# Attention products two groups at a time, an ordered exponential and two store queues in a two-layer transformer kernel

## The chip, the cores and the metric

The kernel runs on one core of a Trainium2 chip. The time is device time in microseconds (us) from the first to the last instruction of the slowest core, as reported for each run; the profile's own span is about 1.7 us shorter. Engine names are those of the profile: PE is TensorE, PEld its weight loads, DVE is VectorE, ACT is ScalarE, POOL is GpSimd, SP is SyncE. A "q" behind a name means the engine's sequencer, for example one that issues a DMA.

## The reference, cut to what matters

```python
def _A_ref(x, wqkv, wo):                  # S=2048, D=1024, H=32 heads of Dh=32
    W, dil = 8, 2                         # each position sees itself and 7 earlier ones, 2 apart
    q, k, v = ...                         # from x @ wqkv
    logits = einsum("bhsd,bhswd->bhsw", q, k at idx) * scale
    attn = _softmax(where(mask, logits, -1e9), axis=-1)
    o = einsum("bhsw,bhswd->bhsd", attn, v at idx)
    return o @ wo

def _B_ref(x, W_gate, W_up, W_down):      # F=3584
    gate = relu(x @ W_gate); up = x @ W_up
    return (gate * up) @ W_down

for _ in range(2):
    x = x + _A_ref(_layernorm(x), ...)
    x = x + _B_ref(_layernorm(x), ...)
```

The products of the sliding-window attention run on VectorE, the large matrix products on TensorE. The kernel cuts the 2048 positions into four blocks of 512 and treats two layer pairs times four blocks as eight "blocks", n = 0 to 7. While TensorE does the gate/up and down products of block n, VectorE does the attention of block n+1.

## The kernel before

Four things matter. First, the gate/up steps. In step j (28 of them per block) TensorE fills one accumulator for the gate and one for the up product. Accumulators lie in PSUM, the memory that TensorE writes its sums to; it is divided into banks. ScalarE turns the gate accumulator into `r`. VectorE multiplies it with the up accumulator into `hT`. An accumulator is free for TensorE again only when its reader is done. There are six of them (`tag="acc"`), and each is one PSUM bank in the compiled program.

```python
psum = ctx.enter_context(tc.tile_pool(name="psum", bufs=6, space=bass.MemoryType.PSUM))
# ... cut
for nm in ("g", "u"):
    acc = psum.tile([P, BLK], F32, tag="acc", name=f"acc_{nm}")
    with pe_group():
        for kc in range(KC):
            mm(acc[:], ...)
    accs[nm] = acc
    if nm == "g":
        r = pool["hid"].tile([P, BLK], BF16, tag="r", name="r", bufs=3)
        tail_act[0] = nc.scalar.activation(r[:], acc[:], ACT.Relu).ins
dv(nc.vector.tensor_tensor, hold["hT"][:, j, :], accs["u"][:], r[:], op=ALU.mult)
```

Second, the attention products. Eight groups per block, four VectorE instructions each, and each instruction needs the one before it:

```python
tt = work.tile([P, W, DG, P], BF16, tag="t", name=f"pv_{n}_{g}")
# ... cut: a_bc and v_sh are views of the softmax and of v
dv(nc.vector.tensor_tensor, tt[:], a_bc, v_sh, op=ALU.mult)
dv(nc.vector.tensor_tensor, tt[:, 0:4], tt[:, 0:4], tt[:, 4:8], op=ALU.add)
dv(nc.vector.tensor_tensor, tt[:, 0:2], tt[:, 0:2], tt[:, 2:4], op=ALU.add)
dv(nc.vector.tensor_tensor, ohm[:, g * DG:(g + 1) * DG, :], tt[:, 0], tt[:, 1], op=ALU.add)
gate[0] = tail_dve[0]
```

Third, the helper `dv`: every VectorE instruction given through it is issued after the one given before (`issue_after` fixes the order; it is not a wait). So the hT products and the attention groups stand in one fixed order, that of the planned times at which the Python code emits them. Instructions that do not go through such a helper are placed by the scheduler of the framework. In the kernel before, the exponential of the softmax was one of these:

```python
nc.scalar.activation(d[:], d[:], ACT.Exp, scale=scale)
```

Fourth, DMAs given through `sp_dma` stand in one order on SyncE's queue. `o_d` is the attention result as it is stored, `oT` the same loaded back in the shape that the output projection needs, `w_o` the weights of that projection, `xnT_b` the transposed input of the gate/up products.

## Time and profile before

| | before |
|---|---|
| time, median of the first 3 runs | 1626.2 us (1625.94 to 1627.49) |
| span of the profiled run | 1624.3 us |
| TensorE, VectorE, ScalarE busy | 99%, 68%, 31% |
| end of the last matmul to the end of the span | 3.3 us |

This is the line of the page for the kernel before with the busy time of each engine, its share of the span and the number of instructions:

```profile
PE 1615.9 (99%) x7618; PEld 785.2 (48%) x7618; DVE 1100.5 (68%) x939; ACT 502.2 (31%) x1051; POOL 250.2 (15%) x220
```

TensorE is the limit, but 99% says little about what is left to gain: the Trainium skill ("Perfetto Trace Analysis", Identifying the Most-Contended Engine) warns that the busy share of pipelined matmuls is a poor measure. A sharper reading takes the start times of all 7618 matmuls, in order, and adds up whatever exceeds the steady pace. For 512 columns this pace is 0.216 us. Beyond the start-up, very little exceeds it. The waits view of the kernel before, for PE alone, has the same events with smaller numbers (each line: who waited, for whom, us in total, times, longest):

```profile
PE acc_g L129 <- DVE hT L103: 1.2, 4, 0.3
PE acc_wo L129 <- DMA oT<-o_d: 0.3, 1, 0.3
PE acc_u L129 <- DVE hT L103: 0.2, 1, 0.2
```

Measured from start to start, each of these six waits costs 0.41 to 0.48 us rather than 0.2 to 0.3. In the profile a matmul of 512 columns lasts 0.379 us, while the next one normally starts 0.216 us after it; the difference, 0.16 us of every loss, lies under the record of the matmul before and does not count as idle there.

The chain of waits (followed back from the last instruction, shares of the span by engine) puts much more on VectorE:

```profile
PE 88%; DVE 10%; issue 1%; DMA 1%; ACT 0%; POOL 0%; DVEq 0%; SPq 0%
```

This must not be read as 10% to be won. The chain passes through VectorE wherever TensorE waited for it, even for 0.3 us, and then follows VectorE's own past for 20 us and more, while TensorE was at work all that time.

Why is hT late? These are lines of VectorE's timeline in the gate/up stage of block 1, others left out (start in us, duration, engine, instruction; in square brackets the idle time before it and what ended it):

```profile
352.13 0.68 DVE L103 TENSOR_TENSOR hT<-acc_u,r 128x512 bf16<-128x512 f32 x1
357.96 1.91 DVE L103 TENSOR_REDUCE ssum<-d 128x128 f32<-128x1024 f32 x1 [5.15 <-ACT d L600]
362.64 2.28 DVE L103 TENSOR_TENSOR pv<-a,vhm 128x4096 bf16<-128x4096 bf16 x1
364.96 1.95 DVE L103 TENSOR_TENSOR pv<-pv 128x2048 bf16<-128x2048 bf16 x2
366.95 0.42 DVE L103 TENSOR_TENSOR ohm<-pv 128x512 bf16<-128x512 bf16 x1
378.37 1.28 DVE L103 TENSOR_TENSOR hT<-acc_u,r 128x512 bf16<-128x512 f32 x2
```

VectorE stands idle for 5.15 us until the exponential (written to `d`) is done. Then it works through groups of 4.65 us with hT products in between. The hT product that starts at 378.37 ends at 379.06, too late for TensorE, which stops until 379.11:

```profile
379.11 1.89 PE L129 MATMUL acc_g<-xnT_b,w_g 128*128 128x512 bf16 x8 [0.31 <-DVE hT L103]
```

### The profile page before, as it was taken

The page shows a single profiled execution, that of the slowest core. Times are in us where ns is not written, and L with a number is a line of the kernel's source. Part 1 is how long each engine was busy: PE and PEld are TensorE (multiplying, and loading weights), DVE is VectorE, ACT ScalarE, POOL GpSimd, SP SyncE. Part 2 cuts the span into 40 slices and gives each one's busy share as a digit, 9 for nine tenths or more (in the row PEclk, how much of TensorE's full clock was granted, in tenths as well). Part 3 has the DMA queues.
Part 4 walks back from the last instruction along what each step waited for, and adds up shares of the span by engine and source line. Part 5 has one row for each costly group of instructions (what it writes and reads, how often), then busy time and mean ns, then how long its engine had stood idle before and what let it go on. Part 6 is the DMA issues. An engine that isn't in the chain of part 4 may idle for free.

```text
span 1624.3 us, 18771 instructions
## 1 busy us (share of the span) xinstructions
PE 1615.9 (99%) x7618; PEld 785.2 (48%) x7618; DVE 1100.5 (68%) x939; ACT 502.2 (31%) x1051; POOL 250.2 (15%) x220
## 2 busy tenths in 40 slices
PE   9999999999999999999999999999999999999999
PEld 6644445444544445444454444544445444444444
DVE  5799899959496777928679286892858928511211
ACT  5754322325240513405134051330513311131110
POOL 2411003201350102201052010520105100000000
PEclk9999999999999999999999999999999999999999
DMA  9579556776579485694757948579574894655451
GB/s 303 105 192 260 167 171 198 194 207 181 156 216 228 155 228 185 182 229 149 226 179 188 241 148 227 160 204 250 164 230 154 200 251 158 207 164 174 156 168 66
DMA packets 398006, 309.39 MB, mean 190 GB/s; under 512 B 167648, under 2 KB 377952, under 8 KB 396256
## 3 DMA queue, kind: packets, MB, share of 16 engines
q1 hardware_dynamic: 397632, 307.81, 67.1%
q8 instruction: 59, 0.97, 0.2%
q10 hardware_dynamic: 288, 0.39, 0.1%
q14 instruction: 27, 0.22, 0.0%
HBM read 263.06 MB, written 27.29 MB: 179 GB/s over the span
## 4 chain that ended last, share of the span: by engine, by line
PE 88%; DVE 10%; issue 1%; DMA 1%; ACT 0%; POOL 0%; DVEq 0%; SPq 0%
PE acc_g L129 21%; PE acc_u L129 20%; PE dacc L129 18%; PE acc_wo L129 7%; PE acc_q L129 6%; DVE pv L103 6%; PE dacc_pair L129 6%; PE acc_k L129 5%; PE acc_v L129 5%; DVE hT L103 1%; DVE ssum L103 1%; DMA x<-in_A_x_dram 1%; DVE prod L103 1%; DVE bst L103 0%; ACT d L600 0%
## 5 line engine op out<-in xcount | busy, mean ns | idle before, releaser
L129 PE MATMUL acc_g<-xnT_b,w_g 128*128 128x512 bf16 x1792 | 423.3, 379 | 1.2 <-DVE hT L103 1.2
L129 PE MATMUL acc_u<-xnT_b,w_u 128*128 128x512 bf16 x1792 | 423.3, 379 | 0.2 <-DVE hT L103 0.2
L711 ACT ACTIVATE r<-acc_g 128x512 bf16<-128x512 f32 x224 | 133.4, 595 | 751.8 <-PE acc_g L129 722.3
L103 DVE TENSOR_TENSOR hT<-acc_u,r 128x512 bf16<-128x512 f32 x224 | 150.0, 687 | 237.7 <-PE acc_u L129 235.5
L129 PE MATMUL dacc<-w_d,hT 128*128 128x512 bf16 (+1 forms) x1400 | 301.6, 375 | 0.0
L129 PEld LDWEIGHTS <-hT 128*128 128x128 bf16 x1820 | 178.2, 98 | 208.9
L129 PEld LDWEIGHTS <-w_g 128*128 128x128 bf16 x1792 | 175.2, 98 | 213.6 <-issue 3.0
L129 PEld LDWEIGHTS <-w_u 128*128 128x128 bf16 x1792 | 175.4, 98 | 211.8 <-issue 0.5
L547 DVE TENSOR_TENSOR t<-q,k 128x2048 f32<-128x2048 bf16 x84 | 191.8, 2292 | 8.7 <-ACT k L482 5.8
L557 DVE TENSOR_TENSOR ac<-ac,t 128x2048 f32<-128x2048 f32 x84 | 191.9, 2285 | 0.3
L103 DVE TENSOR_TENSOR pv<-a,vhm 128x4096 bf16<-128x4096 bf16 x64 | 146.1, 2283 | 0.0
L487 POOL COPY kh<-k 128x14 bf16<-128x14 bf16 x64 | 80.0, 1254 | 398.7 <-ACT k L482 398.7
L748 DVE TENSOR_TENSOR x<-dacc,x 128x512 bf16<-128x512 f32 (+1 forms) x50 | 32.1, 676 | 158.1 <-PE dacc L129 158.1
L103 DVE TENSOR_TENSOR pv<-pv 128x2048 bf16<-128x2048 bf16 (+1 forms) x128 | 122.7, 959 | 4.4
L129 PE MATMUL acc_wo<-w_o,oT 128*128 128x512 bf16 x512 | 111.9, 379 | 0.3 <-DMA oT<-o_d 0.3
L246 POOL TENSOR_TENSOR st_a<-st_a,neg_half 128x1 f32<-128x1 f32 x32 | 49.4, 1551 | 390.7 <-ACT st_a L245 390.7
L129 PE MATMUL dacc_pair<-w_d,hT 128*128 128x512 bf16 x420 | 95.9, 379 | 0.0
L246 POOL TENSOR_TENSOR st_b<-st_b,neg_half 128x1 f32<-128x1 f32 x29 | 47.6, 1650 | 289.9 <-ACT st_b L245 289.9
L129 PEld LDWEIGHTS <-oT 128*128 128x128 bf16 x512 | 49.7, 97 | 61.2 <-DMA oT<-o_d 0.8
L486 POOL COPY k<-kh 128x14 bf16<-128x14 bf16 x48 | 67.5, 1406 | 68.4 <-DVE t L547 43.8
L478 ACT CAST q<-acc_q 128x512 bf16<-128x512 f32 x64 | 37.3, 583 | 75.3 <-PE acc_q L129 75.3
L241 ACT ACTIVATE xn_b<-x 128x1024 bf16<-128x1024 bf16 x29 | 30.3, 1046 | 93.0 <-DVE x L687 78.0
(137 smaller groups left out, 1232.2 us busy)
## 6 DMA issues: line engine op xcount, KB each, us to landing
w_g<-in_B_W_gate_dram SPq DMA_DIRECT2D x56, 1024.0 KB, 6.7
w_u<-in_B_W_up_dram SPq DMA_DIRECT2D x56, 1024.0 KB, 5.5
w_d<-in_B_W_down_dram SPq DMA_DIRECT2D x48, 1024.0 KB, 5.8
w_o<-in_A_wo_dram SPq DMA_DIRECT2D x16, 1024.0 KB, 7.3
vhm<-v_d SPq DMA_DIRECT2D x32, 284.0 KB, 6.8
v_d<-vT SPq DMA_DIRECT2D x8, 1024.0 KB, 10.0
oT<-o_d SPq DMA_DIRECT2D x32, 256.0 KB, 4.3
w_d<-in_B_W_down_dram SPq DMA_DIRECT2D x16, 512.0 KB, 3.9
```

Source lines behind the costliest of these rows:

```text
L103: tail_dve[0] = f(*args, **kwargs).ins
L129: tail_pe[0] = nc.tensor.matmul(*args, **kwargs).ins
L241: nc.scalar.activation(xn, xt[:], ACT.Square, accum_out=sq)
L246: nc.gpsimd.tensor_tensor(rstd, vpe, neg_half[:, 0:1], op=ALU.pow)
L478: tail_act[0] = nc.scalar.copy(q[:], acc[:]).ins
L486: nc.gpsimd.tensor_copy(k[:, 0:HALO], khalo[n - 1][:, c, :])
L487: nc.gpsimd.tensor_copy(khalo[n][:, c, :], k[:, BLK:BLK + HALO])
L547: nc.vector.tensor_tensor(t[:], i0, i1, op=ALU.mult)
L557: nc.vector.tensor_tensor(o, ac[:], t[:], op=ALU.add)
L711: tail_act[0] = nc.scalar.activation(r[:], acc[:], ACT.Relu).ins
L748: nc.vector.tensor_tensor(xs, a[:, c0:c1], xs, op=ALU.add)
```

## The change

Its intent: take two groups in turn, so that no instruction needs the result of the one just before it, and plan the steps 6.0 instead of 6.5 us apart; run the exponential between two fixed gate activations; move the first head reduction (TensorE sums the query-key products over each head) one step later; issue two of the last five stores from ScalarE's queue.

```diff
@@ softmax
-            nc.scalar.activation(d[:], d[:], ACT.Exp, scale=scale)
+            with tc.issue_after(tail_act[0]):
+                tail_exp[0] = nc.scalar.activation(d[:], d[:], ACT.Exp, scale=scale).ins
@@ attention products: steps mults(g0), adds(g0) for g0 = 0, 2, 4, 6
+        def mults(g0):
+                for g in (g0, g0 + 1):
+                    tts[g] = work.tile([P, W, DG, P], BF16, tag="t", name=f"pv_{n}_{g}")
+                    dv(nc.vector.tensor_tensor, tts[g][:], a_bc, v_sh, op=ALU.mult)
+        def adds(g0):
+                for hw in (4, 2):
+                    for g, tt in pair:
+                        dv(nc.vector.tensor_tensor, tt[:, 0:hw], tt[:, 0:hw], tt[:, hw:2 * hw], op=ALU.add)
+                for g, tt in pair:
+                    dv(nc.vector.tensor_tensor, st["o_hm"][:, ...], tt[:, 0], tt[:, 1], op=ALU.add)
@@ gate/up
-                        tail_act[0] = nc.scalar.activation(r[:], acc[:], ACT.Relu).ins
+                        with tc.issue_after(tail_exp[0]):
+                            tail_act[0] = nc.scalar.activation(r[:], acc[:], ACT.Relu).ins
@@ last stores
+                            if half == 1 and t % 2 == 1 and c0 == 0:
+                                nc.scalar.dma_start(dst, xs)
+                            else:
+                                sp_dma(dst, xs)
@@ plan
-    ev.append((t_qk0 + GAP0 * 9.5, reds[0]))
+    ev.append((t_qk0 + GAP0 * 10.5, reds[0]))
-            spread(pv_steps(n + 1), at + 25.0, 6.5)
+            spread(pv_steps(n + 1), at + 25.0, 6.0)
```

More of the change, by code (lines that the diff above doesn't have):

```diff
@@ L107 @@
     tail_act = [None]
+    tail_exp = [None]
     gate = [None]
@@ L629, in pv_steps, with f @@
     def pv_steps(n):
-        b = n % NB
         st = att[n]
-        def f_(g):
+        tts = {}
+        def mults(g0):
             def f():
-                if g == 0:
+                if g0 == 0:
                     st["o_hm"] = big_tile([P, DH, P], f"ohm_{n}")
-                ohm = st["o_hm"]
-                tt = work.tile([P, W, DG, P], BF16, tag="t", name=f"pv_{n}_{g}")
                 a_bc = _ap(st["a"], 0, [[P, W], [0, DG], [1, P]])
-                v_sh = _ap(st["v_hm"], HALO + g * DG * (HALO + P), [[-DIL, W], [HALO + P, DG], [1, P]])
-                dv(nc.vector.tensor_tensor, tt[:], a_bc, v_sh, op=ALU.mult)
-                dv(nc.vector.tensor_tensor, tt[:, 0:4], tt[:, 0:4], tt[:, 4:8], op=ALU.add)
-                dv(nc.vector.tensor_tensor, tt[:, 0:2], tt[:, 0:2], tt[:, 2:4], op=ALU.add)
-                dv(nc.vector.tensor_tensor, ohm[:, g * DG:(g + 1) * DG, :], tt[:, 0], tt[:, 1], op=ALU.add)
+                for g in (g0, g0 + 1):
+                    tts[g] = work.tile([P, W, DG, P], BF16, tag="t", name=f"pv_{n}_{g}")
+                    v_sh = _ap(st["v_hm"], HALO + g * DG * (HALO + P), [[-DIL, W], [HALO + P, DG], [1, P]])
+                    dv(nc.vector.tensor_tensor, tts[g][:], a_bc, v_sh, op=ALU.mult)
+            return f
+        def adds(g0):
+            def f():
+                pair = [(g, tts.pop(g)) for g in (g0, g0 + 1)]
+                for hw in (4, 2):
+                    for g, tt in pair:
+                        dv(nc.vector.tensor_tensor, tt[:, 0:hw], tt[:, 0:hw], tt[:, hw:2 * hw], op=ALU.add)
+                for g, tt in pair:
+                    dv(nc.vector.tensor_tensor, st["o_hm"][:, g * DG:(g + 1) * DG, :], tt[:, 0], tt[:, 1], op=ALU.add)
                 gate[0] = tail_dve[0]
             return f
-        return [f_(g) for g in range(NG)]
+        return [step(g0) for g0 in range(0, NG, 2) for step in (mults, adds)]
     def store_o(n, g0=0, g1=NG):
@@ L751, in f @@
                             col = half * SLAB + c0
-                            sp_dma(out_dram[row:row + P, col:col + c1 - c0], xs)
+                            dst = out_dram[row:row + P, col:col + c1 - c0]
+                            if half == 1 and t % 2 == 1 and c0 == 0:
+                                nc.scalar.dma_start(dst, xs)
+                            else:
+                                sp_dma(dst, xs)
             return f
```

## The prediction

> **What bounds the kernel now.** TensorE. The page gives it 99% of the 1624.3 us span at clock 1.0; its timeline shows a 512-column matmul every 0.216 us almost without a break. The Trainium skill ("Perfetto Trace Analysis", Identifying the Most-Contended Engine) warns that matmul busy share flatters; so I summed start-to-start intervals. After the start-up (9.5 us) only these losses remain that the change can reach:
> - five waits for VectorE in the gate/up stages of blocks 1 to 5, at 379, 566, 767, 968 and 1163 us: 0.41 to 0.48 us each, 2.4 us together with a 0.07 us echo;
> - 0.47 us at 112 us, where the output projection waits for oT;
> - 0.31 us at 43.3 us, where the first head reduction waits for the fourth product;
> - the end: the last result is ready at 1621.49, but its store issues at 1621.76, because SyncE (0.43 to 0.48 us per queued store) comes from the one before. It lands 1.62 us later; then 0.9 us of closing semaphores.
>
> Together 3.4 us, 0.2% of the time. VectorE (68%) and ScalarE (31%) matter only through these waits.
>
> **What the change does, costed.**
> 1. *Exponential.* In blocks 2 to 6 d is ready at 352.2 (first case), but ScalarE runs the exponential at 356.9, behind two more gate activations; VectorE idles 5.15 us before ssum. Ordered between activations 5 and 6 it should run at 352.3 (1.05 us); activation 6 slips from 349.5 to 353.3, its hT to 353.8, and ssum starts near 354.5 instead of 357.96: VectorE is 3.5 us ahead.
> 2. *Pairs.* A dependent VectorE instruction starts 0.034 us after the end of the one before, an independent one 0.082 us before it: 0.117 us per link, three links per group. 4.65 us per group becomes about 4.3; 2.8 us per eight groups. The skill ("VectorE: DVE Perf Modes", The DRAIN you can't avoid) says that semaphores between chained copies cost nothing; this trace's overlaps differ, so I use the trace. hT products wait behind up to 4.4 us of products, as now behind 4.65.
> 3. *Head.* The eight first groups (67.97 to 105.3) are on the chain of waits to oT; ending 2.8 us earlier, oT lands near 109, before PE needs it. The 0.47 us goes.
> 4. *Reduction one step later*: its fourth product is then ready; the 0.31 us goes.
> 5. *Stores* on two queues: the last issues at about 1621.53; 0.2 us.
>
> **How much is critical.** Most of the VectorE time saved is off TensorE's path; the gain is only the listed waits. At 379 PE waits for an hT that ends at 379.06 and was wanted by 378.64: a miss of 0.4 us against 4 us of new lead. Either edit alone would remove it.
>
> **Predicted**: 1626.2 - 2.4 - 0.5 - 0.3 - 0.2 = 1622.8 us; range 1621.4 to 1625.6 (8 in 10). Faster by over 2%: 0.01; within: 0.98; slower: 0.01.
>
> **What would show it.** PE waiting for hT: from 1.4 us to 0 in the waits view. Idle before ssum: from about 5 us to below 1. In the head, group pitch 4.3. oT no longer releases acc_wo. Matmul pace 0.216 unchanged. From the last matmul to the end 0.2 shorter.
>
> **What would make it wrong.** ScalarE now blocks up to 5.6 us on the exponential, so gate accumulators come free later; a PSUM buffer could be missed there and PE wait anew. The buffer assignment may change with the order. In block 1 the exponential delays an activation by about 2.5 us (slack enough, I think). New waits of 0.5 us each in a few blocks would put the time at 1625. A different granted clock would swamp all of it.

## The result, and the profile after

| | before | after |
|---|---|---|
| time, median of 4 runs | 1626.56 us (1625.94 to 1627.49) | 1622.93 us (1622.67 to 1623.05) |
| ratio, 95% interval | | 0.9977 (0.996 to 0.9994) |
| span of the profiled run | 1624.3 us | 1621.2 us |
| TensorE waits for hT, start to start | 2.4 us in 5 places | 0 |
| last matmul to the end of the span | 3.32 us | 3.03 us |

Ratios in this document are the mean time of one kernel's fast runs over the mean of the other's of the same rounds, so they are not quite the ratio of the medians quoted. A second measurement of both (run after_again below) gave 0.9975.

The waits view of PE after the change has no hT and no oT any more. These are all its lines; they belong to the first 10 us:

```profile
PE tp L366 <- DVE xn_first L103: 1.8, 1, 1.8
PE scratch L130 <- DVE ones L298: 1.5, 1, 1.5
PE acc_v L130 <- DVE xnT_first L103: 0.4, 1, 0.4
PE tp L366 <- DVE mean L103: 0.4, 1, 0.4
```

The chain of waits after the change runs through TensorE almost alone. Its share of VectorE, 10% before, is gone for a gain of 0.2%:

```profile
PE 99%; DVE 0%; DMA 0%; issue 0%; POOL 0%; DVEq 0%
```

Lines of VectorE's timeline in the same stage of block 1, after:

```profile
353.38 0.69 DVE L103 TENSOR_TENSOR hT<-acc_u,r 128x512 bf16<-128x512 f32 x1 [1.61 <-ACT r L721]
353.99 1.91 DVE L103 TENSOR_REDUCE ssum<-d 128x128 f32<-128x1024 f32 x1
358.66 4.49 DVE L103 TENSOR_TENSOR pv<-a,vhm 128x4096 bf16<-128x4096 bf16 x2
363.67 3.55 DVE L103 TENSOR_TENSOR pv<-pv 128x2048 bf16<-128x2048 bf16 x4
367.14 0.75 DVE L103 TENSOR_TENSOR ohm<-pv 128x512 bf16<-128x512 bf16 x2
```

The idle time of 5.15 us has become one of 1.61 us in front of an hT product. The sum `ssum` starts 3.97 us sooner; 0.42 us of that is because TensorE itself is that much ahead, so the exponential is worth 3.55 us here (3.5 predicted). A pair of groups takes 8.6 us; in the undisturbed head the pitch per group fell from 4.66 us ((105.22 - 67.97) / 8) to 4.28 us ((102.31 - 68.08) / 8).

The end. These are the store issues of the two kernels, before and then after (SPq and ACTq are the issuing queues):

```profile
1619.13 3.04 SPq L118 DMA_DIRECT2D out_dram<-x  x5
```

```profile
1616.35 2.72 SPq L119 DMA_DIRECT2D out_dram<-x  x3
1617.22 1.54 ACTq L764 DMA_DIRECT2D out_dram<-x  x2
```

Where did the time go, in the two profiles? Matmul losses after the start-up fell by 3.2 us: 2.38 in the gate/up stages, 0.47 at the output projection, 0.31 in the first reduction, 0.04 elsewhere. The tail fell by 0.29 us. Against this, TensorE's first product started 0.43 us later (9.96 against 9.53 us); the first tile of x landed 0.41 us later (3.88 against 3.47 us). Together 3.2 + 0.29 - 0.43 = 3.1 us, which is the difference of the spans.

**The bank margins.** The compiled program tells which PSUM bank each accumulator has. Joined with the trace, this gives for every accumulator the time between the end of the last reader of the bank's earlier tenant and the first matmul of the new one. I call it the margin. In every handover at which TensorE stood waiting for hT it is 0.05 us: the handover itself. Before, the two smallest margins in the gate/up stage of block 1; after, the smallest, and that of the hT product which was late before (tenants named by letter and step, u11 is the up accumulator of step 11):

| kernel | bank handed | freed by hT at | needed at | margin |
|---|---|---|---|---|
| before | u11 to g15 | 379.06 | 379.11 | 0.05: TensorE stands still |
| before | u10 to g14 | 373.81 | 375.19 | 1.37 |
| after | u9 to u13 | 368.49 | 373.04 | 4.55 |
| after | u11 to u15 | 374.09 | 379.94 | 5.85 |

In the whole kernel before, six handovers have a margin of 0.05 us: one in each gate/up stage of blocks 1 to 5, and the echo in the last of these. They are exactly the five waits and the echo of the prediction. In block 6 the hT products are as late, to within 0.01 us from the start of the stage, but the bank of u11 went to u15 instead of g15, and the smallest margin is 0.64 us: no wait. The Trainium skill ("Perfetto Trace Analysis", Optimization Strategy) says that the same gap repeating on the busy engine can mean too little room for the next tile; here it was indeed a buffer, and the margin shows which one and by how much.

### The profile page after: what moved, and what is told of

It reads as the page before. It is cut to its first block, busy times and chain, and to the rows that moved or that the text cites. A ratio compares the mean times of both kernels' runs of the same rounds, so it can differ in the third digit from the quotient of the medians.

```text
span 1621.2 us, 18791 instructions
## 1 busy us (share of the span) xinstructions
PE 1614.1 (100%) x7618; PEld 785.3 (48%) x7618; DVE 1085.2 (67%) x939; ACT 505.4 (31%) x1051; POOL 250.5 (15%) x220
## 4 chain that ended last, share of the span: by engine, by line
PE 99%; DVE 0%; DMA 0%; issue 0%; POOL 0%; DVEq 0%
PE acc_g L130 24%; PE acc_u L130 24%; PE dacc L130 18%; PE acc_v L130 7%; PE acc_k L130 7%; PE acc_q L130 7%; PE acc_wo L130 7%; PE dacc_pair L130 6%; PE L L130 0%; DMA x<-in_A_x_dram 0%; DVE bst L103 0%; PE tp L366 0%; POOL rstd L316 0%; DVE bst L100 0%; DVE xn_first L103 0%
## 5 line engine op out<-in xcount | busy, mean ns | idle before, releaser
L488 POOL COPY kh<-k 128x14 bf16<-128x14 bf16 x64 | 89.0, 1395 | 743.1 <-ACT k L483 743.0
L103 DVE TENSOR_TENSOR pv<-pv 128x1024 bf16<-128x1024 bf16 (+1 forms) x128 | 113.6, 947 | 0.0
L483 ACT CAST k<-acc_k 128x512 bf16<-128x512 f32 x64 | 37.3, 582 | 60.6 <-PE acc_k L130 60.6
```

The lines of the kernel that those rows point to most:

```text
L103: tail_dve[0] = f(*args, **kwargs).ins
L483: tail_act[0] = nc.scalar.copy(k[:, HALO:HALO + BLK], acc[:]).ins
L488: nc.gpsimd.tensor_copy(khalo[n][:, c, :], k[:, BLK:BLK + HALO])
```

## The experiments

Theory A, that of the prediction: the gain is the removal of a few TensorE waits; hT products free PSUM banks too late by 0.4 us, and either main edit gives enough lead. Rivals: B, the exponential does not suffice because VectorE has too much work; C, ScalarE's late gate activations hold the banks; D, the ordered exponential holds up VectorE in block 1; E, the last group of block 1 is cut up by other products and so delays the loads; G, what helps is the new place of the groups in the order; and the plain belief that less VectorE work is less time. All runs gave correct results.

### 1. The exponential alone

```diff
+            with tc.issue_after(tail_act[0]):
+                tail_exp[0] = nc.scalar.activation(d[:], d[:], ACT.Exp, scale=scale).ins
+                        with tc.issue_after(tail_exp[0]):
+                            tail_act[0] = nc.scalar.activation(r[:], acc[:], ACT.Relu).ins
```

> Before plus the ordered exponential alone. Theory A (TensorE waits because the hT product that frees its PSUM bank comes late, and 3.5 us of lead on VectorE is more than the 0.4 us missed): the five waits of acc_g/acc_u for hT fall from 1.4 us in the waits view to 0; the waits for oT (0.47 us start to start) and inside the first reduction (0.31 us) stay; 2.4 us less, ratio 0.9985. Rival B (VectorE has too much work in this stretch, only shorter products help): the waits stay or shrink by less than half, ratio above 0.9993. Idle of VectorE before ssum: from 5.15 us to 0 in blocks 2 to 6, with 1.6 us of idle before the hT in front of it.

Measured: 1625.13 us against 1626.73, ratio 0.9991 (0.9978 to 1.0003). All five hT waits are gone, so B falls. But the medians differ by 1.6 us, not 2.4 (the interval includes 1, so the times alone show no gain); its waits view of PE has something new.

```profile
PE acc_wo L130 <- DMA w_o<-in_A_wo_dram: 0.9, 1, 0.9
PE acc_wo L130 <- DMA oT<-o_d: 0.8, 2, 0.5
```

From start to start these are 0.64 us at 265 us and 1.03 us at 273 us, in the output projection of block 1 (the second oT wait is the one at 112 us, as before). This was not foreseen, and experiments 5 to 7 follow it up.

In the compiled order one can see, without a run, which half of the edit acts. With "the next gate activation after the exponential" alone, the exponential stands behind gate activation 5, as with both halves. With "the exponential after the last activation" alone, it stays behind activation 8, as in the kernel before.

### 2. The pairs alone

```diff
-                dv(...mult...); dv(...add...); dv(...add...); dv(...add...)      # one group
+        return [step(g0) for g0 in range(0, NG, 2) for step in (mults, adds)]
-            spread(pv_steps(n + 1), at + 25.0, 6.5)
+            spread(pv_steps(n + 1), at + 25.0, 6.0)
```

> Before plus the products in pairs and the spacing 6.0 alone; the exponential stays behind gate activation 8. Theory A: three groups earlier in the queue give about 1 us of lead at the hT that was missed by 0.4 us, so the five waits vanish here too, and the oT wait at 112 us vanishes (head pitch 4.3 us per group against 4.65): 2.9 us less, ratio 0.9982. Rival C (the bank is late because ScalarE runs the gate activations up to 4 us late behind the LN statistics, which pairing doesn't change): the five waits stay, only the 0.47 us at 112 us goes, ratio 0.9997.

Measured: 1623.44 us against 1626.73, ratio 0.9983 (0.997 to 0.9997). No hT wait, no oT wait, no w_o wait; the smallest margin behind an hT product is 0.98 us. ScalarE's gate activations are still late behind the statistics (activation 12 runs 2.4 us after its matmuls; in only_exp it was 4.4 us, as in the kernel before with 4.5), and TensorE waits for hT in neither: C falls. The margins agree: behind a gate activation the smallest of the whole kernel is 1.7 us before and 3.8 us after the change.

Two things could have helped instead of the shorter work, and the trace settles both. The order: in the gate/up stage of block 1 three groups' worth of products stand before the late hT product (step 11) in both kernels, three whole groups before, four first products and the sums of two groups here. It ends 52.22 us after the first gate matmul of the stage in before and 51.24 us here. The bank: here the bank of u11 goes to u15, with a margin of 2.29 us. Had it gone to g15, which starts 1.73 us sooner, 0.56 us would have been left, so the lead alone is enough.

### 3 and 4. The later reduction alone; the two store queues alone

```diff
-    ev.append((t_qk0 + GAP0 * 9.5, reds[0]))
+    ev.append((t_qk0 + GAP0 * 10.5, reds[0]))
```

> Before with the first head reduction one step later alone. Expected: the 0.31 us loss between the reduction matmuls at 43.3 us goes, all five hT waits and the oT wait stay; the oT wait may grow by the same 0.3 us if the product chain does not start earlier, in which case nothing is gained at the end: ratio 0.9998 to 1.0.

```diff
-                            sp_dma(out_dram[row:row + P, col:col + c1 - c0], xs)
+                            (the if/else of the change)
```

> Before with the last stores over two queues alone. Expected: from the end of the last matmul to the end of the span 3.0 us instead of 3.3 us, nothing else changed; ratio 0.9998. If the two queues disturbed each other, the last landing would take longer than the 1.62 us of before and the tail would stay at 3.3 us.

Measured: 1626.81 us, ratio 1.0002 (0.9989 to 1.0014), and 1626.8 us, ratio 1.0003 (0.999 to 1.0015), both against 1626.73. By time alone neither is to be seen. The profile of the stores kernel is that of its slowest run (1628.85 us, clock 0.999), and its length has another cause: the granted clock was 0.66 from 10 to 15 us, where 16 matmuls of 256 columns started 0.213 instead of 0.109 us apart (1.7 us in all), and its first product came at 10.52 us, 1.0 us later than in before. In the profiles, the five hT waits are there in both, as expected. The tail of the stores kernel is 3.02 us against 3.31 in the one beside it, so that 0.3 us is real. The loss of 0.31 us inside the reduction, however, appears in only one of the eight profiles with the early reduction, the first profile of before. The later reduction never shows it, but there was mostly nothing to remove. Both runs also had a w_o wait, at 272 and 275 us, of 1.1 and 0.98 us, against 0.04 in the first profile of before, with the same order of instructions in that stretch.

### 5. The kernel before once more

> The kernel before, unchanged, as a null test and as a second profile of the same program. Ratio 1.0000 with an interval of about 0.0013 to each side. Expected in its profile: the five hT waits of 0.41 to 0.48 us again (they follow from the order of instructions), and at about 272 us a wait of 0 to 1.1 us of acc_wo for w_o, which was 0.04 us in the first profile of before and 1.0 to 1.1 us in two kernels that share this stretch with it: if it shows about 1 us here too, the kernel before usually pays it.

Measured: 1628.22 us (1625.87 to 1629.95) against 1627.67 (1626.03 to 1629.87), ratio 1.0002 (0.9989 to 1.0014). The five hT waits came again, each within 0.01 us. This profile has no w_o wait. So the kernel before sometimes pays it and sometimes doesn't, 0 to 1.1 us.

### 6. The exponential alone, but not in block 1

```diff
+            if n == 1:
+                nc.scalar.activation(d[:], d[:], ACT.Exp, scale=scale)
+            else: (as in experiment 1)
```

> The exponential alone, but in block 1 left as it was. Theory D: ordering it in block 1 makes VectorE about 1 us later there (activation 17 runs after the exponential), so the last product of block 1, the store to o_d, the loads of oT and w_o come 1 us later and TensorE pays 1.7 us at 265 and 273 us, which is why only_exp gained 1.6 us and not 2.4. Then here: hT waits 0 as in only_exp, no oT wait at 265 us, the w_o wait back to that of before (0 to 1.1 us), and about 0.6 to 1 us faster than only_exp: ratio 0.9985. Rival: the loads of only_exp were late by chance of the DMA; then the ratio stays at 0.9991.

Measured: 1624.28 us against 1627.67, ratio 0.9981 (0.9969 to 0.9994). No hT wait, and the oT wait at 265 us is gone; the w_o wait is 0.77 us, inside the range of before. (A wait of 0.49 us for `xnT_b` at 140 us is new; see gate2 below.) Theory D, that the ordered exponential holds up VectorE in block 1, shows in one interval, from the first gate matmul of block 0 to the store of block 1's attention result: 117.42 us in before, 117.42 in before_again, 117.42 here, 118.51 in only_exp. The edit costs 1.08 us there. The intervals of the two ratios overlap, so it is the profiles that decide, and the times only agree.

### 7. The logit products of block 2 behind the attention products of block 1

What makes w_o so late in the kernel before? VectorE's timeline of before at the end of block 1's products shows the last group cut up by the logit products of block 2:

```profile
246.09 2.28 DVE L103 TENSOR_TENSOR pv<-a,vhm 128x4096 bf16<-128x4096 bf16 x1
248.29 2.28 DVE L547 TENSOR_TENSOR ac<-q,k 128x2048 f32<-128x2048 bf16 x1
250.50 1.22 DVE L103 TENSOR_TENSOR pv<-pv 128x2048 bf16<-128x2048 bf16 x1
251.63 2.28 DVE L547 TENSOR_TENSOR t<-q,k 128x2048 f32<-128x2048 bf16 x1
253.83 0.68 DVE L103 TENSOR_TENSOR pv<-pv 128x1024 bf16<-128x1024 bf16 x1
254.44 2.28 DVE L557 TENSOR_TENSOR ac<-ac,t 128x2048 f32<-128x2048 f32 x1
256.64 0.41 DVE L103 TENSOR_TENSOR ohm<-pv 128x512 bf16<-128x512 bf16 x1
```

and SyncE's queue then issues the store of the result, the loads of oT and the load of w_o, in this order:

```profile
257.08 0.34 SPq L118 DMA_DIRECT2D o_d<-ohm  x1
260.95 2.85 SPq L118 DMA_DIRECT2D oT<-o_d  x4
263.89 1.08 SPq L118 DMA_DIRECT2D w_o<-in_A_wo_dram  x1
```

The experiment orders the logit products of block 2 behind the last group:

```diff
-                if n == 1:
+                if n in (1, 2):
                     with tc.issue_after(gate[0]):
```

> Before, with the logit products of block 2 ordered behind the last attention product of block 1. Theory E: in before the last group of block 1 is cut up by fp32 products of block 2 (2.28 us each, three of them), ends at 257.05 instead of about 250.7 us, and so holds back the queue that then loads oT and w_o; without that, w_o is issued before 260 us and lands before 267 us, TensorE waits for neither; the five hT waits stay. From 0.0 to 1.1 us less than before, about 0.6 on average: ratio 0.9996. Rival: w_o lands late because of the transfers around it, whatever its issue time; then the wait of about 1 us stays.

Measured: 1626.3 us against 1627.67, ratio 0.9992 (0.9979 to 1.0006). The five hT waits stay, there is no wait for w_o, and its five runs lie within 0.7 us (1625.7 to 1626.41) where the 14 runs of before in the same rounds spread over 4.1 us. The queue of this kernel:

```profile
250.45 0.34 SPq L118 DMA_DIRECT2D o_d<-ohm  x1
254.33 2.93 SPq L118 DMA_DIRECT2D oT<-o_d  x4
258.37 0.37 SPq L118 DMA_DIRECT2D w_o<-in_A_wo_dram  x1
```

w_o landed at 266.29 us, about five us before it is used. The issue time decided, not the transfers around it: the transfer itself took 7.9 us from issue to landing here, longer than the 6.5 us of the lucky run of experiment 5. In the pairs no instruction of block 2 comes between, and they are shorter, so in the changed kernel the store is issued at 248.57 us (109.29 us from the first gate matmul of block 0, against 117.42). That is how the change removes this wait too. The load of w_o goes out at 258.41 us there, no sooner than in gate2: by the waits view it is then held until PE is done with a q product (`acc_q`), and no longer by the store. (The wait for oT at 112 us is missing in gate2's profile as well; its oT landed 3.0 us after the issue instead of 4.2. I did not find out why. And gate2 has a wait of 0.45 us for `xnT_b` at 139 us. Of the fourteen profiles three show such a wait of 0.45 to 0.49 us (exp_not1, gate2, slack4) and two lose 0.2 us at the same place (only_gap, after_again): kernels with and without the pairs, so it falls to chance too.)

### 8. The spacing of the groups alone

```diff
-            spread(pv_steps(n + 1), at + 25.0, 6.5)
+            spread(pv_steps(n + 1), at + 25.0, 6.0)
```

> Before with the spacing of the groups 6.0 instead of 6.5 and nothing else: no pairs. If the place of the groups in the order, and not the shorter dependent links, had taken away the waits in only_pairs, they vanish here too (ratio 0.9985). Expected: the groups come sooner in the order and push the hT products behind them later, so the five waits stay or grow (0.4 to 1.5 us each): ratio 1.000 to 1.003.

Measured: 1632.17 us against 1627.67, ratio 1.003 (1.0017 to 1.0043): slower. Its waits view of PE:

```profile
PE acc_g L129 <- DVE hT L103: 7.0, 5, 1.5
```

So G falls, as far as the spacing goes: the denser plan alone again gives five waits, one per stage, and each is about three times as long (1.5 to 1.6 us from start to start). They are not the same handovers: hT product 9 now stands behind two groups instead of one, and its bank goes to g13, while the late product of before, step 11, ends as it did (52.22 us into the stage). The denser plan is affordable here with the shorter groups. The pairs at the old spacing of 6.5 were not run.

### 9 and 10. The changed kernel again, and without the exponential

> The changed kernel, unchanged, beside the next one on the same chip. Expected: ratio 0.9977 as before, runs within about 1 us of each other (its first four lay within 0.4 us, those of the kernel before within 2 to 4 us), no wait of TensorE for VectorE or for a DMA after the start-up.

```diff
-            with tc.issue_after(tail_act[0]):
-                tail_exp[0] = nc.scalar.activation(d[:], d[:], ACT.Exp, scale=scale).ins
+            nc.scalar.activation(d[:], d[:], ACT.Exp, scale=scale)
```

> The changed kernel without the ordered exponential (pairs, later reduction, two store queues stay). Theory A with slack: pairs alone already reach every PSUM bank in time (smallest margin 0.98 us in only_pairs), so the exponential adds margin and no time: the same time as after_again within 0.5 us, ratio 0.9977, no hT wait. Rival: the exponential brings its own part of the gain even beside the pairs; then this is 1 to 2 us slower than after_again, ratio 0.9985 to 0.999.

Measured on the same chip: 1622.53 us (1622.32 to 1622.9) for the changed kernel, 1622.51 us (1622.36 to 1622.81) without the exponential, ratios 0.9975 and 0.9974 against the same runs of before (1626.72). Beside the pairs the ordered exponential is worth nothing in time. It is worth margin: in the gate/up stage of block 1 the smallest one behind an hT product is 0.98 us without it and 4.55 us with it.

### 11 and 12. More VectorE work on purpose

```diff
-            dv(nc.vector.tensor_reduce, ssum[:], ...)
+            for _ in range(1 if n < 2 else 3):      # 5 in the second kernel
+                dv(nc.vector.tensor_reduce, ssum[:], ...)
```

> The changed kernel with the sum of the softmax computed two more times in blocks 2 to 7 (results unchanged): about 3.9 us more VectorE work before the products in each of six blocks, 23 us in all. The PSUM banks go round as in the changed kernel, whose smallest margin behind an hT product in that stretch is 4.55 us. Expected: no wait of TensorE, the time of the changed kernel within 0.5 us, ratio 0.998. If VectorE's work counted for time here, 23 us more would give ratio 1.012.

> The same with four more sums: about 7.7 us in each of six blocks. This is past the margin of 4.55 us (bank freed by hT of step 9, needed by the up group of step 13) by 3.2 us. Expected: TensorE waits about 3 us for hT in each of the six gate/up stages, 16 to 19 us in all, ratio 1.007 to 1.010. If no wait came, the bank margins would not be what decides.

Measured: 1622.94 us, ratio 0.9976 (0.996 to 0.9991), with two more sums; 1642.94 us, ratio 1.01 (1.0086 to 1.0113), with four. The first has no wait of TensorE after the start-up, and the handover u9 to u13 in block 1 has a margin of 0.65 us left of 4.55. The second shows:

```profile
PE acc_u L130 <- DVE hT L103: 17.2, 18, 1.4
```

From start to start these 18 waits lose 3.31 us in each of five blocks (0.46, 1.55 and 1.29 in block 1) and 3.6 in the other, 20.1 us in all; the median rose by 20.4 us over after_again. VectorE was busy 1085.4 us in after_again, 1107.2 us with two more sums, 1130.1 us with four. The first 22 us of additional work cost nothing, and the next 23 us cost 20. The margin of the bank tells where the one turns into the other.

## Why the prediction was right, point by point

**The time** was 1622.93 us where 1622.8 was predicted, with 1621.4 to 1625.6 as the range. It rested on a list of what TensorE lost, and the large term of that list, 2.4 us, was right in size and cause. That the sum came within 0.2 us of the median is in part luck: 0.3 us of it (the reduction) is not lost in most runs, and a wait that the list lacked, 0 to 1.1 us, makes up for it.

**The five hT waits (2.4 us).** Right in size and cause. The five places were quoted with their losses, all five came again in before_again, only_red, only_stores and gate2, and either main edit removed them (experiments 1 and 2). That PSUM banks freed late by hT decide is shown by the margins and by experiments 11 and 12, where the loss of 3.2 us per block was worked out from the margin beforehand and 3.3 was measured.

**Exponential: 3.5 us of lead.** Right (3.55). But the statement "slack enough, I think" for block 1 was wrong for this edit alone: in only_exp, TensorE lost 1.7 us there for oT and w_o. Leaving block 1 out gave VectorE its 1.08 us back there and removed the oT part. In the full change the pairs cover it.

**Pairs: 0.117 us per link, 4.3 us per group, 2.8 us per eight groups.** Right: 4.28 us, and (4.66 - 4.28) x 8 = 3.0 us. The oT load for block 0 was predicted near 109 us; its first part, the one the first matmul needs, landed at 108.06, and the wait of 0.47 us went. Of the 3.9 us gained there, 2.9 come from the earlier issue (104.85 against 107.79 us) and 1.0 from a shorter time to landing, which the prediction did not count on.

**Reduction: 0.31 us.** Mis-sized as a steady term. It was in the one profile that the prediction read and in none of the seven others with the same order, so as a gain of the median it is near 0.

**Stores: 0.2 us.** It was 0.3.

**What the list lacked.** The wait for w_o in block 1, 0 to 1.1 us from run to run. The profile read beforehand happened to show 0.04 us of it. It can explain part of why the medians fell by 3.6 us in the first measurement and by 4.2 in the second, where the terms summed to 3.4, and of why the runs of before scatter (1625.46 to 1629.95 over all) while the nine of the changed kernel lie between 1622.32 and 1623.05. It can't explain all of a scatter of 4.5 us: the start-up differs too, as the profile of only_stores shows (2.7 us at a clock of 0.66 and a late first product). The two slowest runs of before also have a mean clock of 0.999, but were not profiled. How often the kernel before pays this wait was not measured.

**Most of the VectorE time saved is off the path.** Right, and with a number: 22 us put back cost nothing.

Left open: why oT landed sooner in gate2, why TensorE's first product starts at times that differ by up to a microsecond from run to run, what the wait for `xnT_b` at 139 us depends on, and why the clock was low at the start of one run.

None of the kernels tried was faster than the changed one by more than the noise (no_exp: 1622.51 against 1622.53 us). After the change TensorE has no wait left between the start-up and the tail beyond what a switch of shape costs in the reductions (0.19 to 0.25 us each) and 0.2 us at 139 us in one of its two profiles.

## What to carry to other kernels

On an engine that is never idle, list the losses of the busy engine from start to start before costing a change. The sum of the losses that a change can reach is its whole gain, however much it saves elsewhere. For a producer that is always a little ahead or behind, compute the margin of each buffer handover; it tells in advance how much work another engine can take on for nothing and where the cost sets in. Take several profiles of the kernel before: a wait that falls to chance may be missing in the one that you read, and another may be there by chance.

## What the Trainium skill lacked or had wrong

- "VectorE: DVE Perf Modes", The DRAIN you can't avoid and Rules for kernel authors: it says that chained VectorE instructions cannot avoid the flush, that a semaphore costs nothing there, and advises to reduce the number of instructions rather than the waits. It adds that an instruction that is not "held" starts earlier, but gives no time for it, and its advice leaves it out. Here an instruction that needs the one before it starts 0.034 us after its end, an independent one 0.082 us before its end, also where it waits for a semaphore already reached. Taking two chains in turn cut a group of four from 4.66 to 4.28 us with the same instructions, so not only their number counts.
- "TensorE: Matmul & The Clock Gate", Back-to-back issue gap: it gives about 131 ns per matmul as the sustained pace for 512 columns with weight loads. In all profiles here this pace is 216 ns, which agrees with the page's formula for the isolated gap.
- "DMA: Bandwidth & Descriptors", Issuing engines are not separate DMA queues: it says that issuing from several engines saves only the sequencer's time. This agrees: 0.3 us of tail for five stores (3.3 to 3.0 us). No page gives a figure for what a store that waits costs the loads behind it on the same queue; here it moved w_o by 5.5 us (263.89 against 258.37 us).
- "Perfetto Trace Analysis", Optimization Strategy: the hint that repeating bubbles can mean too few buffers fitted, but the page leads only to the instruction that the engine waits for (hT), not to the buffer, nor to how near the other handovers are to a wait. The margin of each bank handover did (0.05 us where TensorE stood still, 0.64 us where the same lateness met another bank).
